# An attention and feed-forward kernel: its TensorE order, PSUM banks, copy engines and first loads taken from written-out lists instead of a greedy planner

## The chip, the cores and the metric

The kernel runs on one core of a Trainium2 chip. Each core has five engines that run their own instruction streams and meet only through semaphores: TensorE (PE) for matrix products, ScalarE (ACT), VectorE (DVE), GpSimd (POOL) and SyncE (SP), which here only issues DMAs. PE writes to PSUM, a memory of eight banks, from which ACT and DVE copy results into SBUF. The 16 DMA engines serve every queue. The metric is the device time of one execution in microseconds (us), lower is better.

## The reference

The inputs are q, k and v of shape (4 batches, 8 heads, 768 positions, 64) in float32, two weight matrices and a vector beta. First comes attention with a window of 128 positions and four "sink" positions that every query sees:

```python
scores = scale * np.matmul(q, k.transpose(0, 1, 3, 2))
is_sink = pos[None, :] < int(n_sink)          # n_sink = 4
rel = pos[:, None] - pos[None, :]
in_window = (rel >= 0) & (rel < int(window))  # window = 128
scores = np.where(is_sink | in_window, scores, -1000000000.0)
a = np.exp(scores - max) ; a = a / (sum(a) + 1e-09)
x = np.matmul(a, v)                           # then as 3072 tokens x 512
h = x @ w_in                                  # 512 -> 2048
g = h * (1.0 / (1.0 + np.exp(-beta * h)))
out = g @ w_out                               # 2048 -> 512
```

## The kernel before, in words

The work is cut into eight half-batches (`hb` or `T_`, 0 to 7) of 384 tokens, and the attention of each half-batch into four units (`u`, 32 in all), one for each pair of heads. A unit passes through these steps, named here as in the code:

- **load** brings q, k and v in as float32, and **cast** makes bfloat16 copies (`x16`, `vaug`). For half-batch 0 there are four loads each of q and k (q0.0 to q0.3, k0.0 to k0.3, one for each pair of heads, 192 KB) and three of v (v0.0 to v0.2, one for each block of 128 positions, 256 KB). For half-batches 1 and 2, q and k are one load each of 768 KB.
- **T** transposes q and k of a unit on PE (L725); ACT or DVE copies the result to `qkT` (from half-batch 3 on, a DMA transpose does this).
- **S** (`SC`) computes a burst of score tiles on PE (L823). ACT takes the exponentials (L840), DVE or POOL masks them (L848, L854, L858). **SS** or **F** does the same for the sink positions (L870).
- **A** (`AV`) multiplies the weights with v (L926, and L915 for the sinks); DVE takes a reciprocal (L930) and normalizes (L932) into `onorm`. All three v blocks of a half-batch are needed to finish any of its A.
- **R** (`OT`) transposes the result (L952) and ACT or DVE copies it to `xT`, the input of the feed-forward part.

The feed-forward part of a half-batch is 16 **H** groups (`HQ`, four matmuls with w_in, L970; tanh on ACT, L975; product on DVE, L977) and 12 **O** groups (`OQ`, four matmuls with w_out each, L993), then a copy to `osb` and the store. H groups of a half-batch need all four units' `xT`. The weights come in 16 loads of 512 KB, w0 to w7 for w_in and w8 to w15 for w_out, each cast to bfloat16 by ACT, DVE or POOL. w0 and w1 serve two H groups each; after that a pair of loads serves four, so the fifth to eighth H group need w2 and w3.

Nothing of the order is decided on the chip. While the program is made, class `Graph` records operations with `add`, and keeps a simple clock for each engine (`place`): fixed durations, a fixed 180 ns for a hop between engines, one shared DMA time. `_program` chooses the next PE group greedily by that clock (the `while True` loop with `head`), after a short written-out start; `choose` and `take` pick the PSUM banks; `any_of` gives a copy to one of several engines. `background` adds loads, casts and DMA transposes when they come due. Then `Graph.arrange` goes through all operations once more, in order of its clock, and may let PE groups overtake each other; its result is the program order of each engine. Loads that have a `chain` number are linked in the order in which they were added: each becomes available only when the one before has been arranged. `resolve` and `emit` place the semaphores and write each engine's stream.

Until the real work is dense, the `filler` inserts matmuls on a tile of ones (L1212 by the profile) where the clock sees PE idle. Before the change, SP issues all loads but k0.0 to k0.3, which ACT issues. The loads' order is `LOADS`.

Of the kernel before, what the change touches and what calls it, by code (L numbers as in the profile page):

```python
# [16 lines left out]
NM = DF // 128  # L17
# [5 lines left out]
class Op:  # L23
    __slots__ = ("eng", "fn", "deps", "signal", "count", "waits", "sem", "vc", "dma", "seq", "end", "ns", "alts",
                 "group", "tail", "hold", "lock", "chain", "preds", "ready", "left", "succ", "at")


class Graph:
# [6 lines left out]
    HOP = 180  # L35
    SKIP = 3
    PAD = 100
    STRICT = 1
    WIDE, EARLY = 10, 60000
    SLACK = 0  # L40
# [3 lines left out]
    def __init__(self):  # L44
        self.ops = []
        self.writers = {}
        self.readers = {}
        self.last_x = {}
        self.free = {e: 800.0 for e in self.ENGINES}
        self.dma_free = 2500.0  # L50
        self.stalls = [(16000.0, 1100.0), (34000.0, 700.0)]
        self.port = {"gp": 0.0, "dve": 0.0}
        self.group = 0
        self.filler, self.fill_to = None, 0

# [4 lines left out]
    def add(self, eng, fn, ns=0, r=(), w=(), x=(), dma=None, alts=None, after=(), hold=550, chain=None, lock=False):  # L60
# [9 lines left out]
        o.lock = lock  # L70
# [22 lines left out]
        for p, _ in deps:  # L93
            at = max(at, p.end + (0 if p.eng == eng and not p.dma else self.HOP))
# [4 lines left out]
    def fill(self, fn, r):  # L99

        def one():
            o = Op()
            wide = self.free["pe"] + 2 * self.filler[0] <= self.fill_by
            o.eng, o.fn, o.dma, o.ns = "pe", fn[wide], None, self.filler[0] * (1 + wide)
            o.signal, o.count, o.waits, o.vc, o.lock = False, 0, [], None, False
            o.deps = [(p, True) for k in r for p in self.writers[k]]
            return o
        self.filler, self.fill_to = (self.COLD, one), self.group

    def shut(self, o, eng):  # L110

        return self.port["gp" if eng == "dve" else "dve"] if eng == "gp" or eng == "dve" and o.lock else 0.0

    def place(self, o, at):
# [3 lines left out]
        if o.dma:  # L118
# [4 lines left out]
            o.end = self.dma_free + 1000  # L123
        else:
            o.end = self.free[o.eng] = at + o.ns

    def at(self, keys):

        t = 0.0
        for k in keys:  # L130
            ws = self.writers.get(k)
            if not ws:
                return None
            t = max([t] + [p.end + self.HOP for p in ws])
        return t

    def bank_at(self, k):
        return max([0.0] + [p.end + self.HOP for p in self.last_x.get(k, ())])

    def arrange(self):  # L140
# [18 lines left out]
        for o in reversed(ops):  # L159
            o.tail = max([s.tail + self.HOP for s in o.succ] + [0.0])  # L160
# [3 lines left out]
            o.tail += o.ns + (2000 if o.dma else 0)  # L164
        groups = {}
        for o in ops:
            if o.eng == "pe":
                groups.setdefault(o.group, []).append(o)
        todo_pe = list(groups.values())
        self.free = {e: 800.0 for e in self.ENGINES}  # L170
        self.dma_free = 2500.0
        self.stalls = [(16000.0, 1100.0), (34000.0, 700.0)]
        self.port = {"gp": 0.0, "dve": 0.0}
        new, planned = [], set()

        def ready(o, e):
            return max([0.0] + [p.end + (0 if p.eng == e and not p.dma else self.HOP) for p in o.preds])

        def done(o):
            planned.add(id(o))  # L180
            new.append(o)
            for s in o.succ:
                s.left -= 1
                if s.left == 0 and s.eng != "pe":
                    pool.append(s)
            if id(o) in follow:
                s = follow[id(o)]
                s.left -= 1
                if s.left == 0:
                    pool.append(s)  # L190

        pool = [o for o in ops if o.left == 0 and o.eng != "pe"]
        while todo_pe or pool:
            best = None
            wide = self.SKIP if self.free["pe"] > self.EARLY else self.WIDE
            if todo_pe and todo_pe[0][0].group <= self.fill_to:
                wide = self.STRICT
            for i, grp in enumerate(todo_pe[:wide]):
                own = set(map(id, grp))
                if any(id(p) not in planned and id(p) not in own for o in grp for p in o.preds):  # L200
                    continue
                t, off = self.free["pe"], 0.0
                for o in grp:
                    t = max([t] + [p.end + self.HOP - off for p in o.preds if id(p) not in own and p.eng != "pe"])
                    off += o.ns
                if best is None or t < best[0] - self.SLACK:
                    best = (t, "pe", i)
                if t <= self.free["pe"]:
                    break
            by_eng = {}  # L210
            for o in pool:
                opts = []
                for e, (fn, ns) in o.alts.items():
                    t = max(self.free[e], ready(o, e), self.shut(o, e))
                    if o.dma:
                        t = max(t, self.dma_free - 3000)
                    opts.append((t + ns, t, e))
                _, t, e = min(opts)
                by_eng.setdefault(e, []).append((t, o))
            first = {}  # L220
            for e, c in by_eng.items():
                t0 = min(c, key=lambda x: x[0])[0]
                first[e] = (t0, max((x for x in c if x[0] <= t0), key=lambda x: x[1].tail)[1])
# [4 lines left out]
            for e, (t0, o) in first.items():  # L228
# [4 lines left out]
            if e == "pe":  # L233
                grp = todo_pe.pop(what)
                late = t + self.PAD if t > self.free["pe"] + 40 else t
                self.fill_by = late
                while self.filler and grp[0].group <= self.fill_to and self.free["pe"] + self.filler[0] <= late:
                    o = self.filler[1]()
                    self.place(o, max([self.free["pe"]] + [p.end + self.HOP for p, _ in o.deps]))
# [5 lines left out]
                for o in grp:  # L245
                    self.place(o, max([self.free["pe"]] + [p.end + self.HOP for p in o.preds if p.eng != "pe"]))
# [149 lines left out]
def _program(nc, G, sb, ps, q, k, v, w_in, w_out, beta, out):  # L396
# [4 lines left out]
    CUT = 3  # L401
# [42 lines left out]
    WIDE_W, SPL, BQ = 2, ('act','gp'), "sp"  # L444
    EARLY, BST, SOON = 0, [1,2,2]+[3]*5, 2200
    LANES, QUADS = [6,7], [5,7]
    P = ps("P", (128, 8, 512))

    def add(eng, fn, ns, r=(), w=(), x=(), dma=None, after=(), hold=550, chain=None):
        return G.add(eng, fn, ns, r, w, x, dma, None, after, hold, chain)  # L450

    def any_of(alts, r=(), w=(), x=(), lock=False):

        return G.add(min(alts, key=lambda e: G.free[e] + alts[e][1]), None, 0, r, w, x, None, alts, lock=lock)
# [22 lines left out]
    held, reserve = {7}, [False]  # L477
    ring, two = [[6,5,4]], [[0,1],[2,3],[0,1],[2,3],[4,5]]

    def choose(n):  # L480

        if n == 1:
            runs = [[j] for j in (LANES if reserve[0] else range(8)) if j not in held]
            return min([(max(G.bank_at(("B", j)) for j in c), c[0] not in LANES, c) for c in runs], default=None)
        runs = [[]]
        for _ in range(n // 2):
            runs = [r + [i, i + 1] for r in runs for i in range(r[-1] + 1 if r else 0, 7, 2) if not held & {i, i + 1}]
        return min([(max(G.bank_at(("B", j)) for j in c), c[0] in LANES, c) for c in runs], default=None)

    def banks_at(n, more=False):  # L490
        c = choose(n)
        if c and more:
            rest = [G.bank_at(("B", j)) for j in range(8) if j not in held and j not in c[2]]
            return max(c[0], min(rest)) if rest else None
        return c and c[0]

    forced = []

    def take(n):
        if forced:  # L500
            got = [forced.pop(0) for _ in range(n)]
        elif ring[0]:
            if n == 1:
                got = ring[0].pop(0)
                ring[0].append(got)
                got = [got]
            else:
                got = list(range(n))
                if n == 2:
                    got = two.pop(0)  # L510
        else:
            got = choose(n)[2]
# [77 lines left out]
    def load(hb, n, i):  # L590

        b, t0, z = hb // 2, hb % 2 * HALF, hb % NSTG
        if n == "v" or hb >= CUT:
            src = {"q": q, "k": k, "v": v}[n][b, :, t0 + i * 128:t0 + (i + 1) * 128, :].rearrange("h p d -> p h d")
            dst, keys, ns = stg[n][z][:, i, :, :], [("stb", n, z, i)], NV0 if hb < 2 else 1092
        else:
# [4 lines left out]
            ns = NQ0 * len(keys) if hb == 0 else 1950 if hb == 1 else 2080  # L601
            keys = [("stg", n, z, j) for j in keys]
        after = [("stg", n, z, j) for j in range(4)] if hb in range(CUT, CUT + NSTG) and n != "v" else ()
        add("act" if hb == 0 and n == "k" and Q2 else "sp", lambda e: e.dma_start(dst, src), ns, w=keys,
            dma=f"d{n}{z}{'' if i is None else i}", after=after, chain=hb if hb < 3 else None)

    def load_w(j):
# [5 lines left out]
        else:  # L613
            src = w_out_src[:, 2 * (j - 8):2 * (j - 8) + 2, :]
        dst = wst[j % NWS].rearrange("p c f -> p (c f)").rearrange("p (c f) -> p c f", c=4 if j < WIDE_W else 2)
        add("sp", lambda e: e.dma_start(dst, src), 1300 if j < WIDE_W else 1170, w=[("wst", j % NWS)], dma=f"dw{j % NWS}",
            chain=2)
# [6 lines left out]
    def cast_w(j):  # L624
# [13 lines left out]
        any_of(copies(dst, src_, {"act": 947} if j in W0 else {"gp": 1060} if j < 4 else {"act": 947, "dve": 602, "gp": 1060}), r=[("wst", j % NWS)], w=[("w16", m, h)], lock=True)  # L638

    def cast(hb, n, i):  # L640
# [16 lines left out]
        ns = {"act": 413, "dve": 400} if hb == 0 and n != "v" else {"act": 540, "dve": 340, "gp": 612}  # L657
        any_of(copies(dst, src, ns), r=r, w=w, lock=True)
# [44 lines left out]
    def XP(hb, n, c):  # L703
# [7 lines left out]
        for j in range(4):  # L711
# [617 lines left out]
```

## Time and profile before

| what | us |
|---|---|
| median of 3 runs | 221.8 |
| lowest and highest run | 221.3, 223.34 |
| the profiled execution: span from its first to its last instruction | 219.7 |
| PE busy | 213.4 |
| ACT busy | 147.2 |
| DVE busy | 138.1 |
| POOL busy | 75.2 |

The page gives the span of the profiled execution and no other time of it; the runs' times hold what lies around the span too. "PEld" is PE's loading of the stationary operand, which runs beside its matmuls. A name such as "PE L970" is the engine and the line of the kernel; "<-" in a wait stands before what ended it; a "q" behind an engine's name is its instruction queue. In a table by stretch the columns are the stretch, its length, busy time and number of instructions of each engine, the granted PE clock, the share of the DMA engines and GB/s. In a timeline the columns are start, length, engine, line, operation, tiles, shapes and number of instructions.

### The profile page before, as it was taken

To read this page: it belongs to the slowest core of one execution; us is meant where nothing else is said; L and a number is where in the kernel's file an instruction comes from. 1 tells how busy PE (TensorE), PEld (TensorE's weight loads), DVE (VectorE), ACT (ScalarE), POOL (GpSimd) and SP (SyncE) were. 2 spreads that over 40 slices of the span, in tenths; PEclk is the share of its full clock that TensorE was granted. 3 is DMA by queue.
4 is the path that set the end of the run, shared out by engine and by line. 5 is a ranking of instruction groups with operands and counts; after the bars stand their busy time and mean duration, and the time that the engine had idled before them with its cause. 6 is when DMAs were issued, how large, how long until landed. Compare 5 with 4: busy or idle time off the path is not lost.

```text
span 219.7 us, 4563 instructions
## 1 busy us (share of the span) xinstructions
PE 213.4 (97%) x1776; PEld 120.8 (55%) x1793; DVE 138.1 (63%) x293; ACT 147.2 (67%) x241; POOL 75.2 (34%) x140
## 2 busy tenths in 40 slices
PE   8999999999999999999999999999999999999995
PEld 3455557555575575446554556446565456465443
DVE  1697899697774278358960788478886248088000
ACT  2698999586975798459865597275886574187211
POOL 7344551112550790067103770184101770100100
PEclk9999999999999999999999999999999999999999
DMA  6999999999989998499837997659949111400122
GB/s 190 240 302 364 357 287 357 371 298 204 226 185 188 225 141 217 92 253 218 196 74 180 228 182 203 139 142 237 136 98 209 40 63 27 144 2 0 51 95 95
DMA packets 94717, 39.86 MB, mean 181 GB/s; under 512 B 82072, under 2 KB 89512, under 8 KB 94696
## 3 DMA queue, kind: packets, MB, share of 16 engines
q1 hardware_dynamic: 91928, 33.28, 68.9%
q0 software_dynamic: 1680, 5.51, 7.5%
q10 hardware_dynamic: 1088, 0.79, 1.1%
q8 instruction: 14, 0.23, 0.5%
q14 instruction: 7, 0.06, 0.1%
HBM read 27.37 MB, written 6.29 MB: 153 GB/s over the span
## 4 chain that ended last, share of the span: by engine, by line
PE 88%; DVE 6%; DMA 3%; ACT 2%; issue 1%; ACTq 0%
PE P L993 38%; PE P L970 36%; PE P L926 5%; PE P L823 4%; DMA k_stage<-in_k_dram 3%; DVE E L858 2%; PE P L725 2%; PE P L952 1%; DVE g L977 1%; PE P L915 1%; DVE E L848 1%; PE P L870 1%; PE P L1212 1%; DVE w_in L528 1%; ACT E L840 0%
## 5 line engine op out<-in xcount | busy, mean ns | idle before, releaser
L970 PE MATMUL P<-xT,w_in 128*128 128x384 bf16 x512 | 86.8, 327 | 0.4 <-ACT w_in L523 0.2
L993 PE MATMUL P<-w_out,g 128*128 128x512 bf16 (+2 forms) x383 | 84.6, 371 | 1.0 <-issue 0.2
L975 ACT ACTIVATE t<-P,hbeta 128x384 f32<-128x384 f32 x128 | 72.4, 590 | 17.6 <-PE P L970 11.0
L977 DVE SCALAR_TENSOR_TENSOR g<-t,P 128x384 bf16<-128x384 f32 x128 | 67.9, 550 | 21.1 <-ACT t L975 15.7
L970 PEld LDWEIGHTS P<-xT,w_in 128*128 128x128 bf16 x512 | 49.0, 98 | 33.4 <-DVE g L977 0.8
L993 PEld LDWEIGHTS P<-w_out,g 128*128 128x128 bf16 x400 | 37.3, 98 | 40.5 <-issue 0.5
L840 ACT ACTIVATE E<-P 128x1024 bf16<-128x1024 f32 x44 | 43.1, 1036 | 14.1 <-PE P L823 14.1
L854 POOL TENSOR_SCALAR_AFFINE_SELECT E<-E 128x512 bf16<-128x512 bf16 x59 | 38.8, 684 | 27.4 <-ACT E L840 27.2
L1011 POOL DMA_DIRECT2D out_dram<-osb x21 | 11.8, 562 | 63.5 <-ACT osb L523 63.5
L523 ACT ACTIVATE osb<-P 128x512 f32<-128x512 f32 x14 | 8.4, 597 | 25.1 <-PE P L993 25.0
L932 DVE TENSOR_TENSOR onorm<-P,rden 128x384 bf16<-128x384 f32 x32 | 17.6, 554 | 0.8
L529 DVE TENSOR_SCALAR osb<-P 128x512 f32<-128x512 f32 x9 | 6.2, 688 | 15.0 <-PE P L993 14.9
L848 DVE TENSOR_TENSOR E<-E,maskS 128x512 bf16<-128x512 bf16 x16 | 8.8, 564 | 10.4 <-ACT E L840 10.4
L926 PE MATMUL P<-vaug,E 128*128 128x65 bf16 x352 | 15.0, 193 | 0.0
L926 PEld LDWEIGHTS P<-vaug,E 128*128 128x128 bf16 x352 | 14.0, 97 | 1.4 <-ACT E L840 0.4
L823 PEld LDWEIGHTS P<-qkT 64*128 64x128 bf16 x288 | 9.5, 94 | 7.6 <-issue 4.3
L823 PE MATMUL P<-qkT 64*128 64x128 bf16 (+1 forms) x288 | 13.2, 230 | 0.1
L1212 PE MATMUL P<-ones 128*128 128x512 bf16 (+1 forms) x35 | 11.3, 446 | 1.1 <-POOL ones L534 1.1
L528 DVE CAST vaug<-v_stage 128x512 bf16<-128x512 f32 x19 | 9.5, 509 | 3.2 <-DMA v_stage<-in_v_dram 3.1
L697 POOL TENSOR_TENSOR kS<-qkT,headm 128x8 bf16<-128x8 bf16 (+1 forms) x10 | 2.5, 251 | 17.7 <-DMA qkT<-k 9.5
L915 PE MATMUL P<-vS,ES 128*128 128x130 bf16 x40 | 8.1, 221 | 0.4 <-DVE vS L682 0.4
L525 POOL TENSOR_SCALAR_AFFINE_SELECT q<-q_stage 128x512 bf16<-128x512 f32 x7 | 4.8, 693 | 10.4 <-DMA q_stage<-in_q_dram 10.4
(64 smaller groups left out, 119.6 us busy)
## 6 DMA issues: line engine op xcount, KB each, us to landing
v_stage<-in_v_dram SPq DMA_DIRECT2D x24, 256.0 KB, 4.8
out_dram<-osb POOLq DMA_DIRECT2D x21, 256.0 KB, 3.6
q_stage<-in_q_dram SPq DMA_DIRECT2D x15, 256.0 KB, 4.8
k_stage<-in_k_dram SPq DMA_DIRECT2D x15, 256.0 KB, 4.9
wst<-in_moe_w_in_dram SPq DMA_DIRECT2D x5, 512.0 KB, 8.3
wst<-in_moe_w_out_dram SPq DMA_DIRECT2D x4, 512.0 KB, 8.1
g<-in_moe_w_out_dram SPq DMA_DIRECT2D x4, 512.0 KB, 6.6
q_stage<-in_q_dram SPq DMA_DIRECT2D x2, 768.0 KB, 7.8
```

The source lines that it names most:

```text
L528: return lambda e: e.tensor_copy(dst, src)
L823: add("pe", lambda e, dst=dst, kt=kt, kc=kc, rows=rows, q0=q0, nq=nq, u=u: e.matmul(dst, kt[rows, kc:kc + 128], qkT[rows, u % NT, 0, q0:q0 ...
L840: add("act", lambda e, src=src, dst_=dst_: e.activation(dst_, src, AF.Exp, bias=0.0, scale=SCALE), act_ns(1024), w=[("E", z)] + [("m", z, ...
L854: alts = {"gp": (lambda e, dd=dd, sg=sg: e.affine_select(dd, dd, [[0, 4], [sg, 128]], ALU.is_ge, 0.0, base=min(sg, 0), channel_multiplier= ...
L926: e.matmul(A[:, c0:c0 + D + 1], E[t_ % NE][:, i, hh, :], vaug[vz][:, kb % NK, 2 * hp + hh, :], start=a, stop=o, skip_group_check=True), 31,
L932: add("dve", lambda e: e.tensor_tensor(onorm[on][:, :, :, :].rearrange("p m h d -> p (m h) d"), av[:, :, 0:D], rden[on][:, :].unsqueeze(2) ...
L970: add("pe", lambda e, c=c: e.matmul(hp, w_in16[:, c, m * 128:(m + 1) * 128], xT[:, c, t0:t0 + HALF], start=(c == 0), stop=(c == 3)), mm_ns ...
L975: add("act", lambda e: e.activation(tt[ti][:, :], hp, AF.Tanh, bias=0.0, scale=hbeta[:, m:m + 1]), act_ns(HALF) + 93, r=["hbeta"], w=[("t" ...
L977: add("dve", lambda e: e.scalar_tensor_tensor(gt[T_ % NG][:, m, :], tt[ti][:, :], 1.0, hp, ALU.add, ALU.mult), dve_ns(HALF), r=[("t", ti)] ...
L993: add("pe", lambda e, m=m: e.matmul(P[:, bk, 0:n], gt[T_ % NG][:, m, t * 128:(t + 1) * 128], w_out16[:, m, cols], start=(m == 0), stop=(m ...
L1011: add(eng, lambda e: e.dma_start(out_t[3 * T_ + t], osb[z][:, :]), 262144 / 300, r=[("osb", z)], dma=f"do{eng}{z}", hold={"sp": 550, "gp": ...
L1212: G.fill([lambda e, n=n: e.matmul(P[:, 7, 0:128 * n].rearrange("p (a b) -> p a b", a=n), ones[:, :], ones[:, :].unsqueeze(1).to_broadcast( ...
```

## The change: what it does

`_program` now reads two strings. `LOADING` gives the order of the first loads; "@a" sends a load to the ACT queue, the others go to SP. `ORDER` gives the whole sequence of PE groups, with the PSUM banks behind the colon: T1:65 is unit 1's T in banks 6 and 5, S a burst, F a sink group, V and B the first sink values and beta, A, R, H and O as above, and Z ends the filler. The greedy loop, `choose`, `head` and `mark` are gone. `KNOBS` names, for single copies, the engines allowed and an earliest time in the planner's clock. `arrange` takes PE groups strictly in the written order. The planner's clock has hops by pair of engines, and a function `loads` that shares the DMA time between the two queues. What is computed, and the number of matmuls, copies and DMAs of each kind, stays the same; the fillers depend on the clock.

The core of the diff:

```diff
-    HOP = 180
...
+    HOPS = {("act", "dve"): 145, ("act", "pe"): 172, ("act", "gp"): 185, ("dve", "pe"): 147, ("dve", "act"): 140,
+            ("dve", "gp"): 175, ("gp", "pe"): 115, ("gp", "act"): 115, ("gp", "dve"): 115}
+    LATE, LANDED = 205, 30
+    RING, LAG, REACH = 2600, 1150, 1500
+    STALLS = [(5000.0, 750.0), (6500.0, 700.0), (18000.0, 650.0), (36000.0, 500.0), (41000.0, 800.0)]
+    STEP, FIRST = 10.0, 1950.0
...
+    def loads(self, jobs):
+
+        queues = {}
+        for o in jobs:
+            queues.setdefault(o.eng, []).append(o)
...
+                    if left + o.parts <= self.RING and t >= begun[e] + o.hold:
+                        act[e].append([o, self.FIRST if t < 2000 else t + self.REACH, o.ns])
+                        o.due = (begun[e], t)
...
     def place(self, o, at):
...
+        if o.due:
+            o.at = max(at, o.due[0])
+            self.free[o.eng] = max(at, o.due[1])
+            o.end = o.landed + self.LAG
...
         for o in ops:
             if o.chain is not None:
                 if last is not None:
                     follow[id(last)] = o
                     o.left += 1
                 last = o
...
+                    if o.due:
+                        t = max(t, o.due[0])
...
-            for i, grp in enumerate(todo_pe[:wide]):
...
+            if nxt < len(todo_pe) and not open_[todo_pe[nxt][0].group]:
+                best = (starts(todo_pe[nxt]), "pe", None)
...
+    def any_of(alts, r=(), w=(), x=(), lock=False, name=None):
+
+        engs, early = knobs.get(name, ("", "0"))
+        alts = {e: alts[e] for e in alts if not engs or e in [FULL_NAME[c] for c in engs]} or alts
...
-            ns = NQ0 * len(keys) if hb == 0 else 1950 if hb == 1 else 2080
+            ns = 590 * len(keys)
...
-    LOADS = xl(0) + x1[0:1] + x1[1:2] + [0] + [1] + [2] + [3] + [4] + [5] + [6] + x1[4:5] + [7] + x1[3:4] + x1[2:3] + [8] + [9] + [10] + [11] + [12] + [13] + [14] + [15]
...
+    LOADING = "k0.0@a q0.2@a q0.0@a k0.1 q0.1 k0.2@a k0.3 q0.3 v0.1 v0.0 q1 b@a k1 w0 w1 w3 w2 w4 w5 v0.2@a w6 v1.2 w7 v1.1 v1.0 w8 w9 w11 w10 w12 w13 w15 w14"
...
+    consts()
+    for x in LOADING.split():
+        x, _, via = x.partition("@")
+        via = {"": "sp", "a": "act"}[via]
...
```

`KNOBS` begins with `cq0.0=a:0 cq0.1=d:5.8 ck0.1=d:0 cq0.2=d:0 cq0.3=:9.6 cv0.1=dg:14.2 cv0.2=ag:14.9`: the cast of q0.0 goes to ACT, that of v0.2 to ACT or POOL and not before 14.9 us of the planner's clock. `ORDER` begins with

```
T1:65 T0:46 S1:01 T2:24 T3:35 S0:01 S4:45 S2:01 S3:45 V:3 F0:1 B:0 A1:4 A0:0 A3:4 A2:5 R1:1 R3:0 T7:31 Z R0:4 R2:2 T6:17 T5:52 T4:03 H:6 H:7 F1:2 H:3 H:1 S5:5623 H:4 H:7 H:5 S6:0123 H:4 H:6 H:5 H:7 S7:0123
```

The kernel before begins, by its trace, with T0 to T3, S0 to S4 and the sink group between them, A0 to A3, R0 to R3, beta, three T, two H, the last T, two H, S5 with its sink group, three H, S6, four H, S7.

## The prediction

> **What bounds the kernel now.** I read the head of the page first, then the busy time by stretch, PE's waits, and last the timelines of PE, GpSimd, VectorE and SP around 21 us.
>
> ```profile
> span 219.7 us, 4563 instructions
> ...
> PE 213.4 (97%) x1776; PEld 120.8 (55%) x1793; DVE 138.1 (63%) x293; ACT 147.2 (67%) x241; POOL 75.2 (34%) x140
> ```
>
> PE is busy 97%, but a share says nothing on stages. The stretches, cut at PE's first matmul (1.06), its first matmul with w_in (21.17) and its end; the third line is the stretch before 21.17 for L1212 alone, the filler matmuls on `ones`:
>
> ```profile
> 1.06:21.17 20.11, 18.52 (x172) 9.82 (x173) 13.41 (x33) 14.20 (x25) 10.08 (x33) 1.00 1.00 284
> 21.17:217.30 196.13, 194.83 (x1605) 111.03 (x1622) 124.72 (x261) 132.72 (x217) 64.70 (x102) 1.00 0.77 173
> ...
> 1.06:21.17 20.11, 11.25 (x35) 3.58 (x35) 1.00 1.00 284
> ```
>
> Of the first 20.1 us only 18.52 - 11.25 = 7.3 us are work. After 21.17, 194.8 of 196.1 us are busy, and PE's waits from 21 us on are these two:
>
> ```profile
> PE P L970 <- ACT w_in L523: 0.2, 1, 0.2
> PE P L993 <- issue: 0.2, 1, 0.2
> ```
>
> So the end is the start of the feed-forward matmuls plus a fixed amount of PE work. What sets that start, and the stretch behind it (start, length, instruction):
>
> ```profile
> 19.05 0.33 PE L952 MATMUL P<-ident,onorm 128*128 128x128 bf16 x3
> ...
> 21.17 1.46 PE L970 MATMUL P<-xT,w_in 128*128 128x384 bf16 x8 [0.20 <-ACT w_in L523]
> 22.46 0.33 PE L725 MATMUL P<-ident,q 128*128 128x128 bf16 x3
> ...
> 22.80 1.46 PE L970 MATMUL P<-xT,w_in 128*128 128x384 bf16 x8
> 24.20 0.62 PE L823 MATMUL P<-qkT 64*128 64x256 bf16 x14
> 24.87 0.35 PE L870 MATMUL P<-qkT,kS 128*32 128x384 bf16 x4
> ```
>
> ```profile
> 19.16 0.62 POOL L525 TENSOR_SCALAR_AFFINE_SELECT w_in<-wst 128x512 bf16<-128x512 f32 x1 [0.28 <-DMA wst<-in_moe_w_in_dram]
> 21.34 1.06 POOL L525 TENSOR_SCALAR_AFFINE_SELECT w_in<-wst 128x1024 bf16<-128x1024 f32 x1 [1.55 <-DMA wst<-in_moe_w_in_dram]
> 22.66 1.05 POOL L525 TENSOR_SCALAR_AFFINE_SELECT w_in<-wst 128x1024 bf16<-128x1024 f32 x1 [0.26 <-DMA wst<-in_moe_w_in_dram]
> 24.00 1.05 POOL L525 TENSOR_SCALAR_AFFINE_SELECT w_in<-g 128x1024 bf16<-128x1024 f32 x1 [0.30 <-DMA g<-in_moe_w_in_dram]
> ```
>
> Each cast of w_in starts when its load lands. The fourth (w3) ends at 25.05, and the fifth H group, the first to need w2 and w3, starts at 25.15. A start before 21.17 is therefore given back at 25.15 unless the loads land earlier too.
>
> **The change, part by part.**
>
> *Order of PE.* The matmuls are the same. Up to the fifth H group both orders do the same work: eight T, S0 to S5, both SS, four A, four R, four H. T7 only moves from between the H groups to before them (0.34 us, from 22.46 to 22.80). F1 becomes a group of its own: the row L870 inside S5 ends at 25.15, 0.95 after S5 began; alone it switches the array's shape twice more, 0.1 to 0.2, taken as 0.15.
>
> *Stalls behind 25.15.* From 27.76 to 30.73 PE does 16 matmuls of 0.163 us (1.46 us hold 8 with their tail), 2.60 us, and a switch of 0.10: 0.26 is lost. With the smaller gaps near 31.1 and 34.6 that makes some 0.45 us, the most that order, banks and copy engines can win behind the start. Beyond 50 us I find nothing lost, and cost the rest of the order, its banks and the named copy engines at nothing; cover is PE's backlog, and a wrong step there would cost some tenths.
>
> *Loads.* All 16 DMA engines are full (share 1.00 in the first stretch above), so w0 to w3 land when the bytes ahead of them have. One hole exists: in 11.0 to 11.5 the share is 0.51, in 11.5 to 12.0 0.75, some 0.37 us. It follows SP's blocked issue:
>
> ```profile
> 2.85 5.98 SPq L604 DMA_DIRECT2D v_stage<-in_v_dram  x3
> 8.87 0.98 SPq L604 DMA_DIRECT2D q_stage<-in_q_dram  x1
> ```
>
> The third v load takes SP 4.54 us to issue, and q1 waits behind it. One v load fewer on SP may close the hole: 0.0 to 0.4 us won.
>
> *The third v load, v0.2.* This part decides. It goes to the ACT queue, and stands in `LOADING` between w5 and w6. `arrange` links all these loads into one chain in that order, across queues, and hands a load on only once the one before is planned. `loads`, which gives the times, goes queue by queue: it lets v0.2 leave right behind ACT's first five loads, near 3.7 us. So the plan believes in an early landing while the instruction stands in ACT's stream behind everything planned before w5. Where is that? By the planner's constants k1 begins after 1.95 + 8 x 0.59 + 3 x 1.06 + 2.36 + 1.45 (its stalls) = 13.66, and w4 leaves, w5 being next, when k1 is a fifth through: 14.2. That is a place in program order, not a time of the chip. On the chip, ACT's sequencer has passed the waits of that neighbourhood when the scores are done: in the trace the S groups end at 12.9, while ACT runs their exponentials until 15.3. It does run ahead of its engine: DMA issues stand at 1.39 to 2.88 beside a table load of 1.32 to 2.60. Bounds for the issue: 12.8 and 15.0; I take 13.5, nearer the early end for that reason.
>
> From issue to landing: later v loads of the same shape on a quiet DMA show the low end, and a lone 256 KB store beside loads of another queue (93.4 us) the high one:
>
> ```profile
> DMA to landing us min/median/max: 3.2/4.0/4.4
> ...
> DMA to landing us min/median/max: 5.1/5.1/5.1
> ```
>
> With k1 and w0 in full flow I take 4.5, near the second. v0.2 lands at 18.0 (16.0 to 20.1) instead of 12.26. The Trainium skill (DMA: Bandwidth & Descriptors, Queues, rings and completion order) has each DMA engine take turns between its queues packet by packet; by that the ACT queue isn't starved, and the landing stays inside these bounds.
>
> From there: cast 0.62 plus hops 0.2, so 18.8. All four A need v0.2. PE finishes the first A 0.15 later; VectorE then needs a reciprocal and a normalization per unit, in steps of 0.70:
>
> ```profile
> 17.65 0.56 DVE L932 TENSOR_TENSOR onorm<-P,rden 128x384 bf16<-128x384 f32 x1
> 18.13 0.18 DVE L930 RECIPROCAL rden<-P 128x6 f32<-128x6 f32 x1
> 18.35 0.56 DVE L932 TENSOR_TENSOR onorm<-P,rden 128x384 bf16<-128x384 f32 x1
> ```
>
> The last one ends 0.15 + 0.35 + 0.56 + 3 x 0.70 = 3.15 later, 21.95 against 18.91 before. Transpose and copy take 1.15 more (18.91 to ACT's xT copy ending 19.90, and a hop): H0 at 23.1, with T4 to T6 in that gap. Against 21.17 that is +1.93, less T7's 0.34, plus F1's 0.15, less the 0.45 of stalls that vanish as loads run ahead: +1.3. Behind the waiting cast its engine waits too. On GpSimd that costs nothing much (one row of 0.67 between 14.4 and 17.6); on ACT three casts of q (1.67 us from 15.21) and copies slide. Bounds 0 and 1.2; I take 0.5. **Sum: +1.8 us.** Against the profiled span of 219.7 that is 221.5; the page gives no other time for that execution, which lies 2.1 under the median of the runs, 221.8, for work around the span. I carry the difference to the median: **223.6**. By the bounds of landing (16.0 to 20.1) and cast the sum moves by -2.5 to +2.8, and below, w3's cast ends it at 221.8 + 0.15 - 0.45: this case reaches from 221.5 to 226.4.
>
> **Rivals.**
>
> *v0.2 comes in time* (ACT reaches its issue far earlier, or there is slack I don't see). Then w_in's loads bind: the fifth H group at 25.15, or 0.4 earlier if the hole closes, and 0.45 of stalls gone at best: -0.8, 221.0; range 220.7 to 221.8. This is the side that isn't slower. It decides as soon as v0.2 lands before 16.3: H0 is then at 16.3 + 5.1 = 21.4 at the latest, and the fifth H group 3.8 later (25.15 - 21.17 - 0.34 + 0.15), where w3's cast lets it start anyway. For it: all the rest of the start fits. Against: the chain's order.
>
> *The clock drops.* The plan holds no filler for a wait that it doesn't know. PE would idle from about 15 to 18.8. In the trace the first 10 fillers take 4.45 us, 0.43 us each, twice the 0.21 us of a 512-column matmul in the L993 rows: PE starts at half speed and needs some 4 us of work. If that recurs, 4 us at half speed lose 2 us, of which the normalizations hide a little: +1.7, 225.3; range 224.3 to 227. Against: the idle time is bounded by 3.8 us and may be 2. The Trainium skill (TensorE: Matmul & The Clock Gate, Part 1) states that an idle window of some 3.4 us halves the clock and that the window runs freely; the trace's start agrees with its warm-up, the drop no trace here shows.
>
> *The whole start moves up* by over 2 us: 219.0. It needs w3 cast by 23, and 284 GB/s over the same bytes don't allow that.
>
> **How the numbers follow.** About 1%, 2.2 us, is what a measurement of this kernel tells from no change (219.6 to 224.0). Late v0.2: 0.56, of it 0.36 within 1% and 0.20 above. In time: 0.18, within 1%. Clock: 0.20, slower. Start moved up: 0.06, faster. So faster 0.06, same 0.54, slower 0.40. The range leaves out the last case and the tops of the two slow ones: 220.7 to 226.3.
>
> **What would show it.** Right: a DMA issue of v_stage on ACT's queue past 12 us; its cast ending the idle time of its engine near 18; PE idle before the L926 or L915 matmuls; the first L970 near 23; the L970 rows behind it without the 0.26 gap, and nothing between 50 us and the end. The clock rival: L970 matmuls spaced by 0.32 instead of 0.163 for some us. Wrong: v_stage on ACT's queue before 5 us, or the first L970 before 21. A new wait past 50 us would break the claim that the rest costs nothing.

## The result, and the profile after

The changed kernel takes **234.24 us** (median of 4 runs, 233.73 to 234.66); the kernel before, beside it, 221.56. The ratio is 1.0556, 95% interval [1.0514, 1.0598]: 12.7 us slower. The forecast was 223.6, with a range up to 226.3.

The head of the page after, and its busy time of PE:

```profile
span 232.3 us, 4567 instructions
...
PE 216.0 (93%) x1796; PEld 122.2 (53%) x1796; DVE 135.2 (58%) x287; ACT 151.5 (65%) x247; POOL 76.5 (33%) x140
```

The span grew by 12.6 us and PE's busy time by only 2.6: time was lost waiting. The table by stretch, cut as before at PE's first matmul, its first w_in matmul (now 33.09, line L1016) and its end, says in which part (columns: stretch, length, busy time of PE, PEld, DVE, ACT, POOL, granted PE clock, DMA share, GB/s):

```profile
1.06:33.09 32.03, 20.75 (x180) 11.62 (x181) 13.20 (x33) 14.68 (x27) 11.82 (x35) 0.84 0.77 224
33.09:231.00 197.91, 195.21 (x1619) 110.60 (x1616) 122.04 (x255) 136.78 (x222) 64.28 (x100) 1.00 0.75 165
```

The first matmul with w_in came at 21.17 and comes at 33.09: 11.92 us of the 12.6. From there to the end of the span it is 232.3 - 33.09 = 199.2 us, against 219.7 - 21.17 = 198.5. In the first stretch the granted clock is 0.84, and the DMA engines, full before, have a share of 0.77. PE's two longest waits from 20 us on name the cause:

```profile
PE P L972 <- ACT vaug L579: 10.9, 1, 10.9
PE P L1016 <- DVE g L1023: 1.1, 1, 1.1
```

PE's timeline shows it in place, with what follows up to the start of the feed-forward part:

```profile
15.54 0.19 PE L972 MATMUL P<-vaug,E 128*128 128x65 bf16 x1
26.58 0.68 PE L972 MATMUL P<-vaug,E 128*128 128x65 bf16 x9 [10.86 <-ACT vaug L579]
...
33.09 1.46 PE L1016 MATMUL P<-xT,w_in 128*128 128x384 bf16 x8
```

The first A group stops after the matmuls that need v0.0 and v0.1, for 10.86 us. ACT's timeline tells who is late ("ACTq" is its instruction queue):

```profile
13.30 0.39 ACTq L660 DMA_DIRECT2D v_stage<-in_v_dram  x1
13.54 1.10 ACT L886 ACTIVATE E<-P 128x1024 bf16<-128x1024 f32 x1
14.44 0.36 ACT L920 ACTIVATE ES<-P 128x128 bf16<-128x128 f32 x1
25.89 0.63 ACT L579 ACTIVATE vaug<-v_stage 128x512 bf16<-128x512 f32 x1 [11.09 <-DMA v_stage<-in_v_dram]
...
30.71 0.62 ACT L579 ACTIVATE w_in<-wst 128x512 bf16<-128x512 f32 x1
```

v0.2 is issued at 13.30, where the forecast had put it (13.5), but the cast that waits for it starts at 25.89. The instructions of the tile v_stage between 12 and 27 us give the delay itself:

```profile
DMA to landing us min/median/max: 12.6/12.6/12.6
```

The forecast had 4.5 here, 5.1 at most. The last row of ACT's timeline has a consequence of its own: w0's ACT half is cast at 30.71, behind the copy of xT, and only then is the first staging buffer free for w6. SP issues nothing between its last early load and w6:

```profile
13.77 1.17 SPq L673 DMA_DIRECT2D g<-in_moe_w_in_dram  x2
31.42 0.37 SPq L673 DMA_DIRECT2D wst<-in_moe_w_in_dram  x1
```

w6 left at 21.11 in the kernel before. The stretches of 5 us show the whole start at once (columns as above):

```profile
15.00:20.00 5.00, 0.58 (x9) 0.32 (x7) 1.79 (x4) 0.00 (x0) 2.38 (x4) 1.00 1.09 352
20.00:25.00 5.00, 0.00 (x0) 0.00 (x0) 0.00 (x0) 0.00 (x0) 2.09 (x2) 0.52 0.90 296
25.00:30.00 5.00, 3.42 (x42) 2.81 (x43) 2.36 (x7) 2.71 (x5) 0.00 (x0) 0.50 0.01 2
30.00:35.00 5.00, 4.75 (x53) 3.24 (x52) 2.82 (x8) 4.48 (x11) 0.00 (x0) 0.95 0.44 111
```

Between 15 and 25 PE works 0.58 of 10 us; then, when it works again, it does so at half the clock, 0.50; and the DMA engines stand still between 25 and 30, share 0.01. Behind 50 us the only wait of PE that is listed is one of 0.2 us; the kernel before has one of 0.2 there too.

### The profile page after: what moved, and what is told of

The parts are those of the page before. It is cut to its first block, busy times and chain, and to the rows that moved or that the text cites. A ratio compares the mean times of both kernels' runs of the same rounds, so it can differ in the third digit from the quotient of the medians.

```text
span 232.3 us, 4567 instructions
## 1 busy us (share of the span) xinstructions
PE 216.0 (93%) x1796; PEld 122.2 (53%) x1796; DVE 135.2 (58%) x287; ACT 151.5 (65%) x247; POOL 76.5 (33%) x140
## 4 chain that ended last, share of the span: by engine, by line
PE 86%; DMA 5%; DVE 4%; ACT 3%; issue 0%; POOL 0%; POOLq 0%
PE P L1039 36%; PE P L1016 34%; DMA v_stage<-in_v_dram 5%; PE P L972 5%; PE P L1188 4%; PE P L869 3%; PE P L780 2%; ACT E L886 1%; DVE w_in L584 1%; DVE g L1023 1%; PE P L961 1%; ACT qkT L579 1%; DVE osb L585 1%; PE P L998 1%; DVE E L904 1%; PE P L916 1%
## 5 line engine op out<-in xcount | busy, mean ns | idle before, releaser
L1039 PE MATMUL P<-w_out,g 128*128 128x512 bf16 (+2 forms) x400 | 91.1, 371 | 0.2 <-DVE osb L585 0.2
L1016 PE MATMUL P<-xT,w_in 128*128 128x384 bf16 x512 | 90.1, 326 | 1.1 <-DVE g L1023 1.1
L1016 PEld LDWEIGHTS P<-xT,w_in 128*128 128x128 bf16 x512 | 49.0, 98 | 35.7 <-DVE g L1023 1.4
L900 POOL TENSOR_SCALAR_AFFINE_SELECT E<-E 128x512 bf16<-128x512 bf16 x61 | 41.0, 695 | 49.0 <-ACT E L886 48.7
L972 PE MATMUL P<-vaug,E 128*128 128x65 bf16 x352 | 17.1, 198 | 11.0 <-ACT vaug L579 10.9
L972 PEld LDWEIGHTS P<-vaug,E 128*128 128x128 bf16 x352 | 15.8, 101 | 13.9 <-ACT vaug L579 11.0
L976 DVE RECIPROCAL rden<-P 128x6 f32<-128x6 f32 x32 | 5.7, 186 | 20.6 <-PE P L972 20.4
L1188 PE MATMUL P<-ones 128*128 128x512 bf16 (+1 forms) x38 | 12.9, 472 | 1.1 <-POOL ones L590 1.1
L579 ACT ACTIVATE vaug<-v_stage 128x512 bf16<-128x512 f32 x6 | 3.8, 633 | 11.1 <-DMA v_stage<-in_v_dram 11.1
L584 DVE CAST vaug<-v_stage 128x512 bf16<-128x512 f32 x14 | 7.3, 529 | 4.4 <-DMA v_stage<-in_v_dram 4.4
L579 ACT ACTIVATE qkT<-P 128x384 bf16<-128x384 bf16 (+1 forms) x13 | 6.6, 579 | 2.8 <-PE P L780 2.8
```

The lines of the kernel that those rows point to most:

```text
L579: return lambda e: e.activation(dst, src, AF.Copy, bias=0.0, scale=scale)
L900: alts = {"gp": (lambda e, dd=dd, sg=sg: e.affine_select(dd, dd, [[0, 4], [sg, 128]], ALU.is_ge, 0.0, base=min(sg, 0), channel_multiplier= ...
L972: e.matmul(A[:, c0:c0 + D + 1], E[t_ % NE][:, i, hh, :], vaug[vz][:, kb % NK, 2 * hp + hh, :], start=a, stop=o, skip_group_check=True), 31,
L1016: add("pe", lambda e, c=c: e.matmul(hp, w_in16[:, c, m * 128:(m + 1) * 128], xT[:, c, t0:t0 + HALF], start=(c == 0), stop=(c == 3)), mm_ns ...
L1039: add("pe", lambda e, m=m: e.matmul(P[:, bk, 0:n], gt[T_ % NG][:, m, t * 128:(t + 1) * 128], w_out16[:, m, cols], start=(m == 0), stop=(m ...
L1188: G.fill([lambda e, n=n: e.matmul(P[:, 7, 0:128 * n].rearrange("p (a b) -> p a b", a=n), ones[:, :], ones[:, :].unsqueeze(1).to_broadcast( ...
```

## The experiments

Every edit starts from the changed kernel. What each computes stays the same; where fillers are added, the kernel does extra matmuls whose result nobody reads.

**Is it v0.2's place alone?** Only v0.2 moves in `LOADING` (here and below only the part of a string around the edit is shown): to ACT's first loads, or onto SP behind the other two v loads.

```diff
-k0.3 q0.3 v0.1 v0.0 q1 b@a k1 w0 w1 w3 w2 w4 w5 v0.2@a w6
+k0.3 q0.3 v0.2@a v0.1 v0.0 q1 b@a k1 w0 w1 w3 w2 w4 w5 w6
```

> The changed kernel with one word of LOADING moved: v0.2@a stands right behind q0.3, so ACT issues it near 3 us instead of 13.3. Theory A (the late issue is the whole loss): v0.2 lands at 11 to 13, no wait of PE before the first A over 0.5 us, the clock stays full, first L1016 matmul at 19.9 to 21.3, total 220.3 to 222.0, thus level with the kernel before. Rival B (the new order, banks, engines and the other loads lose something of their own): first L1016 at 21 or earlier too, but total over 223.5, with PE waits behind 35 us that the kernel before doesn't have.

```diff
-k0.3 q0.3 v0.1 v0.0 q1 b@a k1 w0 w1 w3 w2 w4 w5 v0.2@a w6
+k0.3 q0.3 v0.1 v0.0 v0.2 q1 b@a k1 w0 w1 w3 w2 w4 w5 w6
```

> The changed kernel with v0.2 on SP behind v0.0, as before the change. Separates the second queue from the place in the chain. Theory A: v0.2 lands near 12.3, q1, k1, w0 as before the change (15.2, 17.6, 19.1); total 220.5 to 222.3, at most 0.5 above the kernel with the early ACT issue. If the ACT queue as such is what hurts, this one is faster than the early ACT issue by over 1 us.

Measured: 221.69 us on ACT, ratio to before 0.9999 [0.9976, 1.0021], and 221.83 us on SP, 0.9995 [0.9973, 1.0016]; before took 221.97. One word of the change makes the whole loss, and all the rest of it (order, banks, engines, the other loads) nets to nothing within 0.25%. The start and what is behind it with v0.2 early on ACT, in the same stretches as above:

```profile
1.06:21.24 20.18, 18.39 (x180) 9.87 (x181) 12.85 (x33) 14.66 (x27) 8.81 (x33) 1.00 1.07 295
21.24:218.00 196.76, 195.46 (x1619) 110.60 (x1616) 121.94 (x255) 136.91 (x222) 67.35 (x103) 1.00 0.79 171
```

The loads do come earlier: w0 lands at 18.03 (17.98 with v0.2 on SP), where before it was 19.10. The first w_in matmul doesn't: 21.24 and 21.18 against 21.17. VectorE's timeline with v0.2 on SP shows what holds it:

```profile
17.60 0.56 DVE L978 TENSOR_TENSOR onorm<-P,rden 128x384 bf16<-128x384 f32 x1
...
18.98 0.56 DVE L978 TENSOR_TENSOR onorm<-P,rden 128x384 bf16<-128x384 f32 x1
```

The last normalization ends at 19.54, and its transposes, copies and the T groups fill the time to 21.18. So the start isn't bound by loads here, but by the chain from the scores over A and the normalizations to xT.

**What would a load between the two places do?** v0.2 stays on ACT and stands between k1 and w0.

```diff
-b@a k1 w0 w1 w3 w2 w4 w5 v0.2@a w6
+b@a k1 v0.2@a w0 w1 w3 w2 w4 w5 w6
```

> The changed kernel with v0.2@a between k1 and w0 in LOADING: ACT issues it some 3 us earlier (near 10 us). It tells how two queues share the DMA engines. Turns packet by packet: v0.2's 256-byte packets alternate with packets of 768 and 1024 bytes (37 and 47 ns) and not of 2048 (91 ns), 64 rounds on each engine take 3.5 to 4.2 us from the first packet, and v0.2 lands at 16 to 19; first L1016 at 21 to 24, total 222 to 226. ACT's queue served only when SP's has drained: landing stays near 25, total over 232.

Measured: 229.92 us, ratio 1.0354 [1.0319, 1.0389]. The issue comes at 10.25, 3.05 us earlier than in the changed kernel, the landing at 21.02, 4.85 earlier, and the time is (1.0556 - 1.0354) x 221.6 = 4.5 us less. The direction was expected, the size was missed: this load too took far longer than any row that the forecast was built on,

```profile
DMA to landing us min/median/max: 10.8/10.8/10.8
```

and w_in's first matmul starts at 29.02. I therefore counted the DMA packet records of both queues in the traces of the two kernels, in slices of 0.5 us (no printed view holds these counts; part 3 of the page has only their sums). Records of 4 bytes are left out. v0.2 has 1024 packets of 256 bytes:

```
kernel        v0.2 issued   first packet   slice      ACT queue packets (256 B)   SP queue packets
changed       13.30         17.44          18.5-19.0     77                          79 of 2048 B
changed                                    21.5-22.0     78                          77 of 2048 B
v0.2 by k1    10.25         14.60          15.5-16.0    121                         121 of 1024 B
v0.2 by k1                                 17.0-17.5    122                         121 of 1024 B
```

Two things make most of the landing's delay. First, 4.1 to 4.4 us pass from issue to the first packet. Second, the two queues then advance packet for packet, one of v0.2's 256 bytes for one of the weight load's 1024 or 2048, so v0.2 gets a fifth or a ninth of the bytes: 1024 packets at some 120 or 78 in half a microsecond are 4.3 or 6.6 us by the count. A few last packets run on for another 1.6 us, to 25.3 in the changed kernel, at about 5 in each half microsecond, and to 20.4 in the other. In the changed kernel that is about a sixteenth of the rate before, as if one of the 16 DMA engines were behind the others; the records don't name the engine, so this stays a guess. From the last packet to the landing it is 0.6 us in both. The Trainium skill (DMA: Bandwidth & Descriptors, Queues, rings and completion order) has each DMA engine take turns between its queues packet by packet, and the counts over half a microsecond agree with equal turns; what I drew from it does not hold, since equal turns between packets of 256 and 2048 bytes are very unequal shares.

**Is the second queue the fault, or the place?** v0.2 goes on SP's own queue, at the same late place. It ran once.

```diff
-w4 w5 v0.2@a w6
+w4 w5 v0.2 w6
```

> The changed kernel with v0.2 at the same late place of the chain, but on SP's queue, behind w5. Tells what the second queue was worth for this load. Turns packet by packet gave v0.2 its last packet on ACT's queue only when w4's and w5's came too, so in SP's line it should land just after w5: w5 at 24.9 to 25.3 (1 us earlier than 26.0, without v0.2's packets between), v0.2 at 26.0 to 26.8, total 234 to 236. If instead the ACT queue as such was slow (its start held back), v0.2 lands earlier here than 25.9 and the total is below 234.

Measured: 235.92 us in one run. v0.2 is issued at 15.13 and lands at 26.17, behind w5 (25.05); on ACT it was 25.87. The queue is worth 0.3 us of landing; the place decides, since behind w5 a load comes after all of w0 to w5 in the one case and beside them at a ninth of the bytes in the other. This kernel differs in the program's own clock: there the wait is known and filled, and PE's end is put at 229.4. For the changed kernel the same clock gives 216.6, as for both kernels with v0.2 early, because it counts v0.2 as landed at 11.43 although its issue stands at 14.74. What the planner cannot see, it can't avoid.

Still, this run is 1.7 us slower than the changed kernel, with a landing only 0.3 later. Its first w_in matmul comes at 34.21, 8.04 after the landing in place of 7.22, and the rest of the span is 200.0 in place of 199.2. Its trace shows two more things. The fillers end at 23.5, and PE then waits far less than in the changed kernel:

```profile
26.88 0.68 PE L972 MATMUL P<-vaug,E 128*128 128x65 bf16 x9 [3.12 <-ACT vaug L579]
```

Yet the granted clock falls here as well: it is 0.93 between 25 and 26, 0.50 from 26 to 32 and 1.00 only from 33 on. And ACT casts its half of w0 at 17.15, ahead of the late cast of v0.2; SP issues w6 at 17.95, and the DMA engines never stop (share 1.17 between 25 and 30, 0.96 between 30 and 35).

**What is the half clock worth?** 50 filler matmuls of 512 columns go in before the first A, so that PE does not idle.

```diff
+        if x == "A" and i == 1:
+            G.begin()
+            for _ in range(50):
+                add("pe", lambda e: e.matmul(P[:, 7, :].rearrange("p (a b) -> p a b", a=4), ones[:, :],
+                                             ones[:, :].unsqueeze(1).to_broadcast([128, 4, 128]), start=True, stop=True),
+                    0, r=["ones"])
```

> The changed kernel with 50 filler matmuls of 512 columns (10.8 us at full clock) ahead of the first A, so that PE doesn't idle while v0.2 is on its way; v0.2 lands late as in the changed kernel. Theory clock: the granted clock stays 1.0, the A, R and T behind the wait run at full speed, first L1016 at 31 to 32 instead of 33.1, total 232 to 233.3. Rival (the half clock is hidden by the normalizations on VectorE and ACT's casts): first L1016 within 0.4 of 33.1 and total 233.8 to 234.6.

Measured: 232.39 us, ratio 1.0467 [1.0438, 1.0496]. v0.2 lands where it did (25.65), and the clock stays whole (columns as above):

```profile
20.00:25.00 5.00, 5.00 (x25) 2.27 (x24) 0.00 (x0) 0.00 (x0) 2.09 (x2) 1.00 0.91 300
25.00:30.00 5.00, 4.58 (x71) 3.08 (x70) 3.20 (x10) 3.77 (x8) 0.00 (x0) 1.00 0.01 4
```

From landing to the first w_in matmul it takes 31.51 - 25.65 = 5.86 us in place of 33.09 - 25.87 = 7.22. The half clock costs 1.6 us by the spans (232.3 - 230.7) and 2.0 by the ratios. (v0.2 lands 0.2 earlier here, which is in both figures; the stretch behind the landing gives 1.36.) It is a part of the loss, not its cause. The DMA engines stand still between 25 and 30 here too, so that has nothing to do with the clock.

**Does the cast on ACT hold back w6?** v0.2's cast is allowed on VectorE alone; then the same with the fillers, in one run.

```diff
-cv0.2=ag:14.9
+cv0.2=d:14.9
```

> The changed kernel with the late cast of v0.2 on DVE instead of ACT (one knob, cv0.2=d:14.9); v0.2 itself lands as late as before, near 25.9. In the changed kernel ACT stands still from 14.8 to 25.9 in front of this cast, with the casts of q1 and k1 and half the cast of w0 queued behind it, so SP can't reuse w0's buffer for w6 before 31.4, and the DMA engines idle from 25 to 31. Theory (this head-of-line blocking on ACT costs of its own): w6 issued at 18 to 21, no idle DMA engines around 28, PE's wait of 1.1 us near 43 gone, total 231.3 to 233.3. Rival (all of the loss sits in the wait for v0.2 and in the chain behind it): w6 early too, but total within 0.7 of 234.2. The planner itself puts this plan 1.9 us later than the changed one, so a smaller gain than 1.5 doesn't settle it.

> The same, and the 50 filler matmuls ahead of the first A that keep the clock. If clock and ACT's blocking add up, 1.6 to 2 below the run with the cast on DVE alone; if both act on the same stretch, less than 1 below.

Measured: 235.15 us, ratio 1.0576 [1.0525, 1.0627], no better than the changed kernel; with the fillers 232.91 in one run, no better than the changed kernel with fillers (232.39). ACT now does the casts of q1 and k1 early, and still w0's half is late:

```profile
15.47 1.22 ACT L579 ACTIVATE k<-k_stage 128x512 bf16<-128x512 f32 x2
30.48 0.49 ACT L579 ACTIVATE xT<-P 128x384 bf16<-128x384 bf16 x1 [13.79 <-PE P L998]
30.87 0.62 ACT L579 ACTIVATE w_in<-wst 128x512 bf16<-128x512 f32 x1
```

ACT idles 13.79 us before the xT copy that waits for PE's transposes, and w0's half stands behind it in ACT's order; SP issues w6 at 31.58. Taking the blocked cast off ACT helps nothing, since the next instruction in its stream waits for the same load by another way. That the order of w0's half on ACT is what delays w6 fits all traces, but no run moved that half alone. The run with v0.2 late on SP comes nearest: with that half ahead of the late cast, w6 leaves at 17.95. The stretch from the first w_in matmul to the end is no shorter there (200.0 against 199.2), so no run shows that w6's delay costs time of its own.

**Is there a version faster than both?** With v0.2 on SP early, VectorE stood idle for 1.29 us at 11.39 to 12.68, and v0.1's cast came after that. The last kernel frees both casts:

```diff
-k0.3 q0.3 v0.1 v0.0 q1 b@a k1 w0 w1 w3 w2 w4 w5 v0.2@a w6
+k0.3 q0.3 v0.1 v0.0 v0.2 q1 b@a k1 w0 w1 w3 w2 w4 w5 w6
-cv0.1=dg:14.2 cv0.2=ag:14.9
+cv0.1=d:0 cv0.2=a:0
```

> v0.2 on SP behind v0.0 (as in the run with v0.2 on SP), and besides v0.1's cast on VectorE and v0.2's on ScalarE may be placed as soon as their loads are in (cv0.1=d:0 cv0.2=a:0 instead of dg:14.2 and ag:14.9). Question: is there a version faster than both kernels once the load is early? Theory 'the held cast': in the run with v0.2 on SP, VectorE stood 1.29 us idle at 11.39-12.68 and did v0.1's cast only at 14.37-15.16, between two of the steps that lead to the last onorm (19.54); moved into the idle gap, the last onorm and the first w_in matmul come 0.4 (its length) to 0.8 us earlier: first w_in matmul 20.4-20.8 in place of 21.18, time 221.0-221.4. Rival 'the exps': the chain is held by ScalarE's exps, which run without a gap from 10.67 to 14.28, and by the transposes before the first w_in matmul; the casts only change places: first w_in matmul 21.1-21.4, time 221.7-222.1, ratio to before 0.999-1.002.

Measured: 221.8 us, ratio 0.9997 [0.9965, 1.0029]. v0.1's cast did move into the gap, and the first w_in matmul came at 20.91, 0.27 us earlier than with the casts held, between what the two theories had. The end didn't follow: the span is 220.4 against 219.5, but these are two single executions, of 222.11 and 221.23 us, and the runs of each kernel spread by more than that. A gain of 0.3 us is below what this measurement can tell. No version tried beats the kernel before.

## Why the prediction was wrong

**The mechanism was right, one term was not.** The order across queues does make ACT issue v0.2 late; the forecast had 13.5 (12.8 to 15.0) for it, measured 13.30. The term that failed is "from issue to landing", taken as 4.5 us from later loads of the same shape and a lone store, bounded by 5.1: it measured 12.57. Neither row had the conditions of this load. The v loads near 91 us came when SP's queue was short (DMA share 0.43 between 92 and 93). The store at 93.4 did run beside full DMA engines, share 1.0 to 1.4, but there the large packets were its own: 64 of 4096 bytes beside SP's 256. Here SP's queue was full of weight loads issued earlier, and it was their packets that were larger, up to eight times. The step "with k1 and w0 in full flow I take 4.5" thus used durations from a short queue, or from the favoured side of the sharing, for the opposite case, and its bound too. Nearer rows stood in the start of the kernel before: the six loads w0 to w5 (512 KB) took 6.7 to 10.2 us there, and the three early v loads, v0.2 itself among them,

```profile
DMA to landing us min/median/max: 7.5/8.0/8.0
```

With 8.0 the landing would have been put at 21.5; even these rows are below the 12.57.

**From landing to H0** the forecast had 5.1 us (18.0 to 23.1). At full clock it is 5.86, so that chain was 0.8 short.

**The clock** was a rival with +1.7 us and a chance of 0.20. It came true, with 1.6 to 2.0. Its argument against (PE idles 3.8 us at most) rested on the same 4.5; PE idled 10.9. And it would not have helped: with v0.2 late on SP the clock fell in a gap of 3.1 us. So the forecast and the rival weren't alternatives: the late load makes both.

**The sum at H0**: forecast 23.1, measured 33.09. Of the 9.99 us between them 7.87 are v0.2's landing (25.87 - 18.0), 1.36 the clock (7.22 - 5.86) and 0.76 the chain. The 2.1 us that carried the forecast from the span to the runs' median were 0.4 too many as work around the span: here as in the runs with v0.2 early the time of the profiled execution is 1.7 above its span (234.03 against 232.3); the rest was the runs' spread.

**Behind H0** the forecast was -0.34 for T7, +0.15 for F1, -0.45 for stalls and +0.5 for the blocked engine, together -0.14; measured +0.7 (199.2 against 198.5). With v0.2 early it is +0.3 (220.0 - 21.24 = 198.8), which single executions can't tell from nothing. The stalls between 25 and 35 do go, as said, and come back as a new one, as the stretches of that kernel show:

```profile
25.00:30.00 5.00, 5.00 (x44) 2.97 (x45) 4.96 (x11) 5.00 (x9) 1.65 (x2) 1.00 1.19 291
30.00:35.00 5.00, 4.99 (x63) 3.27 (x62) 4.80 (x11) 4.91 (x10) 3.74 (x5) 1.00 0.81 237
35.00:40.00 5.00, 4.61 (x55) 2.68 (x52) 4.61 (x13) 3.29 (x5) 0.70 (x1) 1.00 1.03 381
```

The kernel before has PE busy 4.91, 4.89 and 4.95 here. The 0.19 won before 35 is spent at 35 to 40, where PE waits 0.4 us for the cast of w_out. In the changed kernel PE has a wait of 1.1 at 43 us, where VectorE, busy throughout 40 to 45, casts weights that came late; a wait for the same product on VectorE is there in every profile in which v0.2 is late (1.1 with the fillers and beside k1, 0.7 with the cast on VectorE, 1.2 with v0.2 late on SP), and not in the two in which v0.2 alone is moved early. That the blocked engine makes it is not shown: with v0.2 late on SP the weights came early, and the wait is there all the same.

**What held.** "Beyond 50 us nothing lost, the rest of the order at nothing" is borne out by the two kernels with v0.2 early, within 0.25%. The rival "v0.2 in time" gave 221.0 (220.7 to 221.8) on condition that it lands before 16.3; with landings at 10.73 and 11.62 the runs gave 221.69 and 221.83, at the upper end of its range (0.03 above it for the second). It is the time of the change without its fault, save that its reason was off: I had w_in's loads bind the start then, and it is the chain of normalizations and transposes.

**What wasn't thought of**: the DMA engines standing still from 25 to 30. It needs no term of its own in the sum, as the loads had run ahead (GpSimd had cast up to its fourth piece by 23.9), but it spends that lead. That the lead is worth nothing that shows here, the run with v0.2 late on SP suggests: its DMA engines never stop, and its end comes no sooner.

## What to carry to other kernels

When a load moves to another queue, ask three things: behind what its issue stands in the program, what the other queue has in flight at that moment, and how its packet size compares with that of the other queue; a small-packet load beside large packets gets a share by packets, not by bytes. A planner that shares DMA time between queues must take a load's earliest time from the place of its issue in the engine's program, or it will order a wait that it never sees. When a load is late, price what idles with it in the same sum: here the clock. The next loads were late too, at no cost that a run shows.

## What was not expected of the hardware

- A 256 KB load on ACT's queue beside weight loads on SP's took 12.6 us from issue to landing, and 10.8 in another kernel; the quickest of three near 91 us in the kernel before took 3.2. Of that 4.1 to 4.4 us passed before the first packet. Both times the first packet came 0.2 to 0.4 us after those of the last SP load whose issue had ended by then (w3's at 17.23, w0's at 14.24). ACT's first load of the changed kernel, issued at 0.81, had its first packet after 1.8 us, so the delay isn't the same at all times; whether it is a place behind what the DMA engines had already taken up stays open, no run tells.
- The packets of two queues went one to one over 4.3 and 6.6 us, at 256 bytes against 1024 and 2048, so the small-packet queue moved about 40 GB/s beside 315 in the changed kernel (20 KB and 158 KB in the slice 21.5 to 22.0).
- PE idled from 15.7 us; the granted clock is 1.00 in 15 to 20, 0.52 in 20 to 25, 0.50 in 25 to 30 and 0.95 in 30 to 35. It fell some 4.5 us after the work stopped and rose some 4 us after it began again at 26.58. With v0.2 late on SP it fell some 2 us after the work stopped at 23.76 and rose some 6 us after it began again at 26.88. The Trainium skill (TensorE: Matmul & The Clock Gate, Part 1) has an idle window of some 3.4 us halve the clock; the changed kernel agrees in kind, and shows the price, 1.6 to 2.0 us for one such gap, but in the other run a gap of 3.1 us was enough.
